# Attention and two gated layers on one core: the attention weights' transposition and product, three of eight last products, and one scale operand are changed

## The chip, the cores and the metric

The kernel runs on one core of a Trainium2 chip. The metric is the device time of one launch in microseconds (us). The engines are named as in the profile: PE is TensorE (matmuls; PEld is its weight load), DVE is VectorE, ACT is ScalarE, POOL is GpSimd, SP is SyncE, which here only issues DMAs. Each engine takes its own instructions strictly in their written order, and waits on semaphores for the others.

## The reference

Attention of 12288 queries over 768 pooled keys (keys and values are the same matrix), then two layers of width 2048, the first with a leaky ReLU of its own slope for each column, the second with a rational function.

```python
kv_pool = kv.reshape(B, H // r, r, W // r, r, C).mean(axis=(2, 4))      # 768 x 128
k = v = kv_pool.reshape(B, -1, C) @ w_sr
s = (q @ k.transpose(0, 2, 1)) / np.sqrt(C)
a = np.exp(s - s.max(-1, keepdims=True))
a /= a.sum(-1, keepdims=True) + 1e-09
x = a @ v                                                               # 12288 x 128
h = x @ w_in                                                            # 128 -> 2048
x = (np.maximum(h, 0.0) + alpha * np.minimum(h, 0.0)) @ w_out           # 2048 -> 128
h = x @ w_in2
P = a[0] + a[1]*h + a[2]*h*h + a[3]*h*h*h
Q = 1.0 + np.abs(b[0]) * np.abs(h) + np.abs(b[1]) * h*h
out = (P / (Q + 1e-6)) @ w_out2
```

## The kernel before

The work is cut in three streams that run beside each other for most of the launch.

**Attention.** 96 tiles `t` of 128 queries. A tile's scores are two halves of 384 keys (`S_half`), DVE writes them negated with the running minimum (`S_neg`), ACT takes the exponential (`S_exp2`), and POOL multiplies by the reciprocal sum (`norm`). The normalized weights `e` (128 queries x 768 keys) then have to stand with the keys on the partitions. PE transposes them in six blocks of 128 (`T_pe`, three into one bank), ACT copies each three twice, to `aTh` (rounded to the type fp32r) and to `tf` (`T_hi`), and POOL subtracts to get the rest `aTl` (`T_lo`). Two tiles make a pair `g` (48 pairs). The product with the values (`AV`) is done in three terms for each of six blocks of keys, `vh*aTh`, `vh*aTl`, `vl*aTh`, 18 matmuls of 256 columns to a pair (`mm3`, which records lines 381 to 383). The first 12 tiles (`EARLY`) run with their own banks while the weights are prepared; there DVE subtracts and POOL has no part in it.

**First layer.** 24 chunks of 512 queries, each with 16 steps of 128 hidden columns: `G1a` (three fp32r matmuls of 512), ReLU on ACT, a split by ACT and POOL in 11 of 16 steps, and `G2a` (three fp32r matmuls, or one f32 matmul in the five other steps; an f32 matmul of 512 columns stands as two records of the trace).

**Second layer.** 192 pairs of steps `s`: `G1b` on PE, then on ACT `act_u` (absolute value) and `act_p1` (a3*h + a2), on POOL two operations to the denominator, on ACT a logarithm and an exponential, on DVE `dve_e`, `dve_p2`, `dve_p3`, `dve_gr`, and a last product. That is `dve_g` on DVE or, where `by_pool` says so, `act_f` on ACT and `pool_g` on POOL. Then comes `G2b`, an f32 matmul for each step, and each chunk leaves by a DVE transposition in blocks of 32 x 32 and four DMAs to a pair.

**What sets the order.** Every operation is an `Op` with an engine, a cost, a rank and its dependencies. `emit_in_time` goes through a planned time: it takes the operation that can start first, and by rank where several can, and writes it out. So each engine's order is fixed when the program is built, from the costs and from tables of numbers (`TR`, `WR`, `RT`, `RA`, `RB`, `SPREAD`, `LH`, `LM`, `LT`, `RK`). Buffers are rings (`BUFS`, `Ring`): `S` is one bank that holds in turn score halves, transposed weights and the AV product; `e` has 4 buffers. `add(..., port=True)` keeps DVE operations apart from POOL ones in the planned time.

Of the kernel before, what the change touches and what calls it, by code (L numbers as in the profile page):

```python
# [8 lines left out]
F32 = mybir.dt.float32  # L9
# [12 lines left out]
B = 32  # L22
LN2 = 0.6931471805599453
# [173 lines left out]
def kernel(  # L197
# [37 lines left out]
    GEND = (0, 1, 1, 1, 1, 0, 1, 1, 1, 0, 1, 1, 0, 1, 0, 1, 0, 0, 0, 0)  # L235
    FIRST = 0
    LAST = 0
    WR = (46.7, 55.28, 111.13, 125.65, 140.69, 248.67, 278.77, 278.99, 302.55, 429.42, 352.76, 380.94, 597.47, 591.71, 462.41, 295.52)
    TR = (21.24, 22.34, 24.58, 34.83, 72.31, 76.18, 101.27, 117.78, 121.37, 122.99, 130.89, 131.26)
    LH = (137.96, 75.92, 55.11)  # L240
    LM = 45.18
    LT = (44.51, 44.83, 42.99)
    TLO = (1, 1)
    XLO = 0
    TLE = (0, 0)
# [11 lines left out]
        relu=-99.63, G2a=43.29, u=46.57, p1=63.42, t=89.27, ln=107.53, ex=141.17, e=225.02, p2=69.42, p3=50.3, gr=-124.79, g=40.13, f=67.85, gp=39.2, G2b=28.14, gs=13.78, q=27.79,  # L257
# [3 lines left out]
        qraw=True, qf=1, qT=2, S=1, nm=4, sm=4, r=4, e=4, aT=2, xf=1, tf=3, x0=3,  # L261
# [33 lines left out]
    vh = const.tile([P, KB, P], F32R, name="vh")  # L295
    vl = const.tile([P, KB, P], F32R, name="vl")
# [69 lines left out]
    shared = dict(SHARE, qTh="qT", qTl="qT", aTh="aT", aTl="aT", x1h="x1", x1l="x1")  # L366
# [37 lines left out]
    with tc.manual_schedule():  # L404
# [131 lines left out]
        def kT_mm(h):  # L536
            ps = st["kT", h] = new("ps", "S2", [P, HK])
            nc.tensor.matmul(
                out=ps, lhsT=st["wsr"], rhs=st["pooled"][:, h * HK : h * HK + HK], start=True, stop=True
            )  # L540

        def kT_hi(h):
            copy(kTh[:, h * HK : h * HK + HK], st["kT", h], sc)

        def kT_lo(h):
            sl = slice(h * HK, h * HK + HK)
            nc.vector.scalar_tensor_tensor(
                out=kTl[:, sl], in0=st.pop(("kT", h)), scalar=sc, in1=kTh[:, sl],
                op0=ALU.mult, op1=ALU.subtract,
            )  # L550
# [20 lines left out]
        for b in range(KB):  # L571
# [4 lines left out]
            a = add("ACT", act_us(P), 31, lambda b=b: copy(vh[:, b, :], st["v", b]), p)  # L576
            l = add(
                "DVE", dve_us(P), 31,
                lambda b=b: nc.vector.tensor_tensor(
                    out=vl[:, b, :], in0=st.pop(("v", b)), in1=vh[:, b, :], op=ALU.subtract  # L580
                ), a,
            )
            d.append(l)
            v_ops += [a, l]

        def prep_small():
# [3 lines left out]
            nc.vector.tensor_scalar(out=nav, in0=av, scalar1=-1.0, scalar2=None, op0=ALU.mult)  # L590

# [6 lines left out]
        ]  # L598

# [293 lines left out]
        def T_pe(t, j, ring):  # L893
            ps = A["T", t, j] = new("aps", ring, [P, 3, P])
# [5 lines left out]
        def tlo(t, j):  # L900
            return (TLE if t < EARLY else TLO)[j]
# [11 lines left out]
        def T_lo(t, j):  # L913
            g, k = divmod(t, 2)
            sl = (slice(None), slice(None), slice(k * P, k * P + P))
            eng, src = (nc.gpsimd, "tf") if tlo(t, j) else (nc.vector, "T")
            eng.tensor_tensor(  # L917
                out=A["aTl", g, j][sl], in0=A.pop((src, t, j)), in1=A["aTh", g, j][sl],
                op=ALU.subtract,
            )  # L920

        def AV(g, part, ring):
            if part == 0:
                A["av", g] = new("aps", ring, [P, 2 * P])
            ah, al_ = A.pop(("aTh", g, part)), A.pop(("aTl", g, part))
            for k in range(3):
                b = 3 * part + k
                mm3(
                    A["av", g], vh[:, b, :], vl[:, b, :], ah[:, k, :], al_[:, k, :],
                    start=(b == 0), stop=(b == KB - 1),  # L930
                )

# [73 lines left out]
        def transposes(t):  # L1006
            rank = tile_rank(t) + RT
            ring = "T" if t < EARLY else "S"
            g, k = divmod(t, 2)
            n, d_e = s_ops.pop(t)  # L1010
            if k == 0:
                T_ops[g] = [[], []]
            for j in range(2):
                p = add("PE", 0.33, rank, lambda j=j: T_pe(t, j, ring), n)
                d_e.append(p)
                d = rings[ring].take(p)
# [533 lines left out]
```

## Time and profile before

| | |
|---|---|
| median of 3 runs | 1523.71 us (1522.19 to 1524.54) |
| span of the profiled execution | 1521.4 us; this is its own time, from the first to the last instruction, and the page gives no other |
| PE busy | 1482.4 us (97%) |
| DVE busy | 1433.0 us (94%) |
| ACT busy | 1424.4 us (94%) |
| POOL busy | 1326.4 us (87%) |
| mean granted TensorE clock | 0.993 of 2.4 GHz |

Four engines stand near the span, so the share over the whole span does not tell which of them the others wait for. The page's slices show that the first two fortieths and the last are different from the rest: there every engine has gaps. In the stretches between, PE's row has no gap, and the others' have. A PE record's duration overlaps with the next one's, so what a matmul costs is read from the distance between two starts and not from its duration.

### The profile page before, as it was taken

What the parts mean: (1) busy time and instruction counts of PE and PEld (TensorE: products, weight loads), DVE (VectorE), ACT (ScalarE), POOL (GpSimd) and SP (SyncE); (2) the same over time, 40 slices, a digit from 0 to 9 for tenths busy, and PEclk for the clock granted to TensorE, in tenths of its full rate; (3) what the DMA queues carried; (4) which work ended last, traced back from release to release, by engine and by line L of the source; (5) the groups of instructions that cost most, each with busy time, mean ns of one, the idle gap of its engine ahead of it and who ended that gap; (6) DMA issues with size and microseconds to landing.
All of it is one profiled execution on the core that took longest, in us unless ns stands there. A gap on an engine that the chain in (4) does not pass through costs nothing.

```text
span 1521.4 us, 20213 instructions
## 1 busy us (share of the span) xinstructions
PE 1482.4 (97%) x6372; PEld 1065.0 (70%) x6372; DVE 1433.0 (94%) x2161; ACT 1424.4 (94%) x2488; POOL 1326.4 (87%) x1005
## 2 busy tenths in 40 slices
PE   6899999999999999999999999999999999999995
PEld 5777777777777777767777776777777776777652
DVE  5999999999999999999999999999999999999996
ACT  3969999999999999999999999999999999999996
POOL 0258999999999999989999989899999898899997
PEclk9999999999999999999999999999999999999997
DMA  8320000000000000000000000000000000000000
GB/s 285 91 63 0 8 14 1 15 14 1 15 10 5 14 8 8 14 8 8 14 1 15 5 10 15 1 14 8 8 14 8 0 8 8 1 8 8 1 14 7
DMA packets 102411, 28.65 MB, mean 19 GB/s; under 512 B 92960, under 2 KB 99744, under 8 KB 102304
## 3 DMA queue, kind: packets, MB, share of 16 engines
q1 hardware_dynamic: 102192, 27.35, 7.7%
q8 instruction: 50, 0.82, 0.2%
q0 software_dynamic: 112, 0.01, 0.1%
q14 instruction: 57, 0.47, 0.1%
HBM read 21.05 MB, written 6.29 MB: 18 GB/s over the span
## 4 chain that ended last, share of the span: by engine, by line
PE 86%; DVE 5%; ACT 4%; POOL 3%; issue 1%; DMA 1%; SPq 0%; DVEq 0%; POOLq 0%; ACTq 0%
PE acc L1302 20%; PE h L381 11%; PE h L383 11%; PE h L382 11%; PE acc L1157 6%; PE acc L381 4%; PE acc L383 4%; PE acc L382 4%; PE S L381 4%; PE S L382 4%; PE S L383 4%; PE S L898 4%; DVE work L615 1%; POOL work L1263 1%; POOL work L1210 1%
## 5 line engine op out<-in xcount | busy, mean ns | idle before, releaser
L1210 POOL TENSOR_TENSOR work<-work 128x1024 f32<-128x1024 f32 x192 | 460.4, 2398 | 8.0
L1302 PE MATMUL acc<-work,wo 128*128 128x512 f32 x768 | 393.7, 600 | 10.1 <-POOL work L1263 9.4
L1196 ACT ACTIVATE work<-h,nav 128x512 f32<-128x512 f32 x384 | 319.4, 840 | 2.2 <-PE h L383 1.2
L1141 POOL TENSOR_TENSOR rl<-work,rh 128x512 fp32r<-128x512 f32 x216 | 281.0, 1301 | 38.0 <-ACT rh L1132 34.7
L1240 DVE SCALAR_TENSOR_TENSOR work<-work,nav,h 128x512 f32<-128x512 f32 x384 | 281.8, 741 | 4.0
L1236 DVE TENSOR_TENSOR work<-work,h 128x512 f32<-128x512 f32 x384 | 258.8, 679 | 22.8 <-ACT work L1196 21.4
L1203 POOL TENSOR_SCALAR work<-work,bab 128x1024 f32<-128x1024 f32 x192 | 231.4, 1205 | 36.3 <-ACT work L1191 21.4
L1191 ACT ACTIVATE work<-h 128x512 f32<-128x512 f32 x384 | 247.0, 646 | 11.5 <-PE h L383 9.0
L1230 DVE SCALAR_TENSOR_TENSOR work<-work,rp 128x1024 f32<-128x1024 f32 x192 | 233.2, 1214 | 21.7 <-ACT rp L1223 19.3
L1248 DVE SCALAR_TENSOR_TENSOR rp<-work,nav,rp 128x1024 f32<-128x1024 f32 x181 | 231.6, 1280 | 0.0
L1120 ACT ACTIVATE work<-h 128x512 f32<-128x512 f32 x336 | 215.1, 640 | 13.5 <-PE h L383 11.1
L1269 DVE SCALAR_TENSOR_TENSOR work<-work,rp 128x1024 f32<-128x1024 f32 x181 | 219.6, 1213 | 1.8
L1215 ACT ACTIVATE work<-work 128x1024 f32<-128x1024 f32 x192 | 213.9, 1114 | 7.0 <-POOL work L1210 5.0
L1223 ACT ACTIVATE rp<-work 128x1024 f32<-128x1024 f32 x192 | 207.7, 1082 | 8.2 <-DVE work L1269 3.7
L381 PE MATMUL h<-x,w1h 128*128 128x512 f32 x384 | 202.4, 527 | 2.3 <-ACT work L1120 1.2
L381 PE MATMUL h<-x1h,w2h 128*128 128x512 f32 x384 | 187.1, 487 | 3.8 <-DVE work L1240 3.8
L1302 PEld LDWEIGHTS acc<-work,wo 128*128 128x128 f32 x768 | 141.3, 191 | 61.8 <-issue 26.3
L917 POOL TENSOR_TENSOR aTl<-tf,aTh 128x384 fp32r<-128x384 f32 x168 | 170.2, 1019 | 9.4 <-ACT tf L386 9.1
L383 PE MATMUL h<-x1h,w2l 128*128 128x512 f32 x384 | 151.8, 395 | 0.0
L383 PE MATMUL h<-x,w1l 128*128 128x512 f32 x384 | 151.7, 395 | 0.0
L382 PE MATMUL h<-x1l,w2h 128*128 128x512 f32 x384 | 151.3, 394 | 0.0
L382 PE MATMUL h<-x,w1h 128*128 128x512 f32 x384 | 151.1, 393 | 0.0
(138 smaller groups left out, 3226.2 us busy)
## 6 DMA issues: line engine op xcount, KB each, us to landing
work<-in_kv_dram SPq DMA_DIRECT2D x12, 512.0 KB, 8.7
out_dram<-work SPq DMA_DIRECT2D x184, 32.0 KB, 1.6
qraw<-in_q_dram SPq DMA_DIRECT2D x80, 64.0 KB, 2.3
work<-in_moe_w_out_dram SPq DMA_DIRECT2D x8, 512.0 KB, 4.4
work<-in_moe_w_in_dram SPq DMA_DIRECT2D x8, 512.0 KB, 4.5
qraw<-in_q_dram SPq DMA_DIRECT2D x4, 256.0 KB, 2.9
out_dram<-work SPq DMA_DIRECT2D x2, 128.0 KB, 1.8
work<-in_w_sr_dram SPq DMA_DIRECT2D x1, 64.0 KB, 7.9
```

Source lines behind the costliest of these rows:

```text
L381: nc.tensor.matmul(out=ps, lhsT=wh, rhs=xh, start=start, stop=False)
L382: nc.tensor.matmul(out=ps, lhsT=wh, rhs=xl, start=False, stop=False)
L383: nc.tensor.matmul(out=ps, lhsT=wl, rhs=xh, start=False, stop=stop)
L1141: nc.gpsimd.tensor_tensor(out=E["rl", s], in0=E.pop(("r1", s)), in1=E["rh", s], op=ALU.subtract)
L1191: nc.scalar.activation(out=E["u", s][:, k, :], in_=E["h2", s + k], func=AF.Abs)
L1196: nc.scalar.activation(out=E["p1", s][:, k, :], in_=E["h2", s + k], func=AF.Identity, scale=nav[:, 3:4], bias=nav[:, 2:3],)
L1210: nc.gpsimd.tensor_tensor(out=t, in0=t, in1=E.pop(("u", s)), op=ALU.mult)
L1230: nc.vector.scalar_tensor_tensor(out=t, in0=t, scalar=QEPS, in1=E["r0", s], op0=ALU.add, op1=ALU.mult)
L1236: nc.vector.tensor_tensor(out=p, in0=p, in1=E["h2", s + k], op=ALU.mult)
L1240: nc.vector.scalar_tensor_tensor(out=p, in0=p, scalar=nav[:, 1:2], in1=E.pop(("h2", s + k)), op0=ALU.add, op1=ALU.mult,)
L1248: nc.vector.scalar_tensor_tensor(out=E["gr", s], in0=p, scalar=nav[:, 0:1], in1=r, op0=ALU.add, op1=ALU.mult)
L1302: nc.tensor.matmul(out=E["acc2", i], lhsT=wo[2][:, KEEP[2].index(j), :], rhs=E["g", s][:, k, :], start=st_, stop=sp,)
```

## The change

The change takes the transposition of the normalized weights off PE, ACT and POOL for tiles 12 to 95. DVE transposes `e` in blocks of 32 x 32 in one instruction of 768 elements (`T_dve`), and four DMAs on SP's queue bring the blocks to their partitions (`T_place`). To make these DMAs contiguous, the keys are numbered otherwise from the pooling on (`kv_out`, `kT_mm`, `kT_hi`). The first 12 tiles still go through PE, with one ACT copy each and no subtraction.

The AV product has one f32 matmul in place of three fp32r ones: 6 to a pair in place of 18. `vl` is gone.

`by_pool` says yes for three of eight pairs of steps (`GPAT`) outside the last 20, where `GEND` decided before and still does with other entries. In all it is 75 of 192 pairs after and 11 before.

`act_p1` takes its scale from a register of ScalarE, loaded once, in place of a column of `nav`.

All tables that set the order have other numbers, and `FPAT` has the same eleven split steps at other places.

```diff
-    RT = 12.37
-    RA = 14.54
-    RB = 119.19
-    SPREAD = 30.17
+    RT = 23.26
+    RA = 19.89
+    RB = 256.57
+    SPREAD = 25.96
...
+    GPAT = (0, 1, 0, 0, 1, 0, 0, 1)
...
-        def T_hi(t, j):
-            g, k = divmod(t, 2)
-            if k == 0:
-                A["aTh", g, j] = new("at", "aTh", [P, 3, 2 * P], F32R)
-                A["aTl", g, j] = new("at", "aTl", [P, 3, 2 * P], F32R)
-            copy(A["aTh", g, j][:, :, k * P : k * P + P], A["T", t, j])
-            if tlo(t, j):
-                A["tf", t, j] = new("at", "tf", [P, 3, P])
-                copy(A["tf", t, j], A.pop(("T", t, j)))
...
+        def T_dve(t):
+            A["eb", t] = new("at", "eb", [P, NK])
+            nc.vector.transpose(out=A["eb", t], in_=A.pop(("e", t)))
+
+        def T_place(t):
+            to, eb = land(t), A.pop(("eb", t))
+            for a in range(W4):
+                nc.sync.dma_start(
+                    out=to[:, a].rearrange("p k i -> p (k i)"),
+                    in_=eb[a * B : a * B + B].rearrange("j (w n) -> j w n", w=W4),
+                )
...
-            for k in range(3):
-                b = 3 * part + k
-                mm3(
-                    A["av", g], vh[:, b, :], vl[:, b, :], ah[:, k, :], al_[:, k, :],
+            for b in range(3 * part, 3 * part + 3):
+                nc.tensor.matmul(
+                    out=A["av", g], lhsT=vf[:, b, :], rhs=A["eT", g][:, :, b, :],
                     start=(b == 0), stop=(b == KB - 1),
                 )
...
-                scale=nav[:, 3:4], bias=nav[:, 2:3],
+                scale=a3_reg, bias=nav[:, 2:3],
...
-            return k < len(GEND) and GEND[k]
+            return GEND[k] if k < len(GEND) else GPAT[s // 2 % len(GPAT)]
```

The order on PE in the middle of the program, before: `h` is a first product (`G1a` or `G1b`), `acc` a second one, and `S<-aTh,vh` begins an AV product.

```order
L381 MATMUL h_7545<-x1h,w2h 128x512
L382 MATMUL h_7545<-x1l,w2h 128x512
L383 MATMUL h_7545<-x1h,w2l 128x512
L1302 MATMUL acc_7032<-work,wo_67 128x512
L381 MATMUL S<-aTh,vh 128x256
L382 MATMUL S<-aTl,vh 128x256
L383 MATMUL S<-aTh,vl 128x256
```

Five more such threes follow there before the next `h`. PE after the change, at an AV product of the same stretch:

```order
L381 MATMUL h_6720<-x_5652,w1h 128x512
L382 MATMUL h_6720<-x_5652,w1h 128x512
L383 MATMUL h_6720<-x_5652,w1l 128x512
L938 MATMUL S<-eT,vf 128x256 x3
L381 MATMUL h_6737<-x1h,w2h 128x512
L382 MATMUL h_6737<-x1l,w2h 128x512
L383 MATMUL h_6737<-x1h,w2l 128x512
L938 MATMUL S<-eT,vf 128x256 x3
```

The 18 short matmuls have become two threes of f32 matmuls with a first product between them, and no `S<-ident,e` (a transposition) stands in the stretch any more. The first of the six waits for the DMAs of both tiles.

The order on DVE in the middle, before: a score pass (`e,nm<-S`), the steps of the second layer, and the last product (line 1269).

```order
L1248 SCALAR_TENSOR_TENSOR rp<-work,nav,rp 128x1024
L863 TENSOR_SCALAR e,nm<-S,nm 128x384
L1269 SCALAR_TENSOR_TENSOR work<-work,rp 128x1024
L877 TENSOR_SCALAR r<-sm 128x1
L882 RECIPROCAL r<-r 128x1
L445 STREAM_TRANSPOSE qf<-qraw 128x512
L1236 TENSOR_TENSOR work<-work,h_6796 128x512
L1240 SCALAR_TENSOR_TENSOR work<-work,nav,h_6796 128x512
```

DVE after the change; line 1264 is the old 1248, and where it writes `work` in place of `rp` the last product that followed is POOL's.

```order
L1246 SCALAR_TENSOR_TENSOR work<-work,rp 128x1024
L1264 SCALAR_TENSOR_TENSOR work<-work,nav,rp 128x1024
L1252 TENSOR_TENSOR work<-work,h_6176 128x512
L924 STREAM_TRANSPOSE eb<-e 128x768
L1256 SCALAR_TENSOR_TENSOR work<-work,nav,h_6176 128x512
L1252 TENSOR_TENSOR work<-work,h_6184 128x512
L1256 SCALAR_TENSOR_TENSOR work<-work,nav,h_6184 128x512
```

A last product of 1024 elements is missing behind line 1264, and a transposition of 768 stands among the steps.

The order on SP's queue in the middle, before (each `x4` is one load of queries in blocks, each `x8` the results of a chunk):

```order
L436 DMA qraw_4366<-in_q_dram 32x16x32 x4
L1340 DMA out_0_dram<-work_88 32x8x32 x8
L436 DMA qraw_5152<-in_q_dram 32x16x32 x4
L1340 DMA out_0_dram<-work_88 32x8x32 x8
L436 DMA qraw_5618<-in_q_dram 32x16x32 x4
```

SP's queue after the change:

```order
L929 DMA eT_4516<-eb_4510 128x1x192 x4
L1356 DMA out_0_dram<-work_87 32x8x32 x8
L929 DMA eT_4819<-eb_4671 128x1x192 x4
L929 DMA eT_4819<-eb_4798 128x1x192 x4
L436 DMA qraw_5002<-in_q_dram 32x16x32 x4
L929 DMA eT_5076<-eb_4956 128x1x192 x4
```

Four DMAs for each tile (336 in all) now stand between the loads of queries and the results, in one queue that is worked off in order. At the queue's head one load of `moe_w_in` now stands ahead of the first loads of `q` and `kv`.

## Rows read from the trace of the kernel before

**Rows 1.** The page's part 1: span, busy time of each engine.

```profile
span 1521.4 us, 20213 instructions
PE 1482.4 (97%) x6372; PEld 1065.0 (70%) x6372; DVE 1433.0 (94%) x2161; ACT 1424.4 (94%) x2488; POOL 1326.4 (87%) x1005
```

**Rows 2.** Windows: stretch, length, busy of PE, PEld, DVE, ACT, POOL, clock, DMA.

```profile
150.00:1450.00 1300.00, 1300.00 (x5555) 934.60 (x5554) 1248.59 (x1842) 1260.47 (x2196) 1201.32 (x906) 1.00 0.05 9
800.00:850.00 50.00, 50.00 (x218) 36.33 (x217) 49.36 (x75) 49.14 (x86) 46.26 (x35) 1.00 0.07 11
```

**Rows 3.** Timeline of PE, two short stretches: start us, duration us, line, operation.

```profile
615.60 1.02 PE L1302 MATMUL acc<-work,wo 128*128 128x512 f32 x2
616.46 0.49 PE L898 MATMUL S<-ident,e 128*128 128x128 f32 x3
616.70 0.48 PE L381 MATMUL acc<-rh,wo1h 128*128 128x512 f32 x1
617.02 0.39 PE L382 MATMUL acc<-rl,wo1h 128*128 128x512 f32 x1
617.25 0.40 PE L383 MATMUL acc<-rh,wo1l 128*128 128x512 f32 x1
...
655.84 0.28 PE L381 MATMUL S<-aTh,vh 128*128 128x256 f32 x1
655.96 0.28 PE L382 MATMUL S<-aTl,vh 128*128 128x256 f32 x1
656.08 0.28 PE L383 MATMUL S<-aTh,vl 128*128 128x256 f32 x1
```

**Rows 4.** Groups by line: shapes and count, busy us, mean ns, idle before.

```profile
L1230 DVE SCALAR_TENSOR_TENSOR work<-work,rp 128x1024 f32<-128x1024 f32 x192 | 233.2, 1214 | 21.7 <-ACT rp L1223 19.3 <-POOL aTl L917 0.8 <-POOL work L1210 0.3
L1236 DVE TENSOR_TENSOR work<-work,h 128x512 f32<-128x512 f32 x384 | 258.8, 679 | 22.8 <-ACT work L1196 21.4 <-ACT work L1191 0.6
L1269 DVE SCALAR_TENSOR_TENSOR work<-work,rp 128x1024 f32<-128x1024 f32 x181 | 219.6, 1213 | 1.8
L917 DVE TENSOR_TENSOR aTl<-T,aTh 128x384 fp32r<-128x384 f32 x24 | 12.9, 547 | 0.4 <-ACT aTh L386 0.2
L1196 ACT ACTIVATE work<-h,nav 128x512 f32<-128x512 f32 x384 | 319.4, 840 | 2.2 <-PE h L383 1.2 <-POOL work L1263 0.6 <-DVE rp L1248 0.4
L1191 ACT ACTIVATE work<-h 128x512 f32<-128x512 f32 x384 | 247.0, 646 | 11.5 <-PE h L383 9.0 <-POOL work L1210 1.0
L386 ACT ACTIVATE tf<-S 128x384 f32<-128x384 f32 x168 | 92.3, 549 | 0.0
L386 ACT ACTIVATE aTh<-S 128x384 fp32r<-128x384 f32 x168 | 90.6, 539 | 1.4 <-PE S L898 1.4
L1259 ACT ACTIVATE work<-work 128x1024 f32<-128x1024 f32 x11 | 11.8, 1077 | 0.8 <-DVE work L1230 0.8
L917 POOL TENSOR_TENSOR aTl<-tf,aTh 128x384 fp32r<-128x384 f32 x168 | 170.2, 1019 | 9.4 <-ACT tf L386 9.1
L1263 POOL TENSOR_TENSOR work<-work 128x1024 f32<-128x1024 f32 x11 | 26.1, 2380 | 1.4 <-ACT work L1120 1.0 <-DVE work L1248 0.4
```

**Rows 5.** One line's instructions: count, duration ns min/median/max, first and last start.

```profile
L445 DVE STREAM_TRANSPOSE qf<-qraw x20: 691/703/712, 69.6 to 1188.4; 128x512 f32<-128x512 f32 x20
...
L615 DVE TENSOR_SCALAR work<-work x48: 399/420/1922, 27.8 to 134.5; 128x512 int32<-128x512 int32 x32, 128x512 f32<-128x512 f32 x16
```

**Rows 6.** Timeline of DVE and POOL around one transposition.

```profile
401.17 1.04 POOL L917 TENSOR_TENSOR aTl<-tf,aTh 128x384 fp32r<-128x384 f32 x1
...
401.85 0.70 DVE L445 STREAM_TRANSPOSE qf<-qraw 128x512 f32<-128x512 f32 x1
```

**Rows 7.** The page's DMA issues (KB each, us to landing), and an issue.

```profile
out_dram<-work SPq DMA_DIRECT2D x184, 32.0 KB, 1.6
qraw<-in_q_dram SPq DMA_DIRECT2D x80, 64.0 KB, 2.3
...
1480.02 1.93 SPq L1340 DMA_DIRECT2D out_dram<-work  x4
```

More of the change, by code (lines that the diff above doesn't have):

```diff
@@ L22 @@
 B = 32
+W4 = P // B
 LN2 = 0.6931471805599453
@@ L575 @@
             d_pooled.append(p)
[L576 to L584, printed above, removed]
+            a = add("ACT", act_us(P), 31, lambda b=b: copy(vf[:, b, :], st.pop(("v", b))), p)
+            d.append(a)
+            v_ops.append(a)
         def prep_small():
@@ L598 @@
         ]
+        a3_op = add(
+            "ACT", 0.2, 7, lambda: nc.scalar.reg_load(a3_reg, nav[0:1, 3:4].bitcast(I32)), small[0]
+        )
         def f64_to_f32(src, k, dst, rank, dst_ring=None):
@@ L1011, in transposes @@
             if k == 0:
[L1012 to L1016, printed above, removed]
-                h = add("ACT", act_us(HK) * (1 + tlo(t, j)), rank, lambda j=j: T_hi(t, j), p)
-                if k == 0:
-                    d_aT[g, j] = rings["aT"].take(h)
-                else:
-                    h.after(T_ops[g][j][0])
-                eng = "POOL" if tlo(t, j) else "DVE"
-                l = add(eng, tt_us(eng, HK), rank, lambda j=j: T_lo(t, j), h)
-                if tlo(t, j):
-                    rings["tf"].take(h).append(l)
-                last = h if tlo(t, j) else l
-                d.append(last)
-                T_ops[g][j] += [h, l]
-        d_aT = {}
+                T_ops[g] = []
+            if t < EARLY:
+                first = None
+                for j in range(2):
+                    p = add("PE", 0.33, rank, lambda j=j: T_pe(t, j), n)
+                    d_e.append(p)
+                    d = rings["T"].take(p)
+                    h = add("ACT", act_us(HK), rank, lambda j=j: T_copy(t, j), p, first)
+                    d.append(h)
+                    first = first or h
+                    T_ops[g].append(h)
+            else:
+                x = add("DVE", dve_us(NK), rank, lambda: T_dve(t), n)
+                d_e.append(x)
+                d_eb = rings["eb"].take(x)
+                first = add("SP", 1.6, rank, lambda: T_place(t), x)
+                d_eb.append(first)
+                T_ops[g].append(first)
+            if k == 0:
+                d_eT[g] = rings["eT"].take(first if t >= EARLY else T_ops[g][0])
+                lead_T[g] = T_ops[g][0]
+            else:
+                (first if t >= EARLY else T_ops[g][-2]).after(lead_T.pop(g))
+        d_eT, lead_T = {}, {}
         def outputs(g):
@@ L1429, in moe2 @@
                 p1 = add(
-                    "ACT", act_us(w, ptrs=2), stage(st, "p1"), lambda k=k: act_p1(s, k), g1, *p3s
+                    "ACT", act_us(w, ptrs=1), stage(st, "p1"), lambda k=k: act_p1(s, k), g1, a3_op, *p3s
                 )
```

86 lines of the change are left out of this document (47 added, 39 removed).

## The prediction

> **What bounds the kernel now.** I read the page's busy times first [rows 1]. PE has 1482.4 of 1521.4 us, DVE 1433.0, ACT 1424.4, POOL 1326.4: four engines within 13 points, so the page alone does not name the bound. The windows do [rows 2]. From 150 to 1450 us PE is busy for 1300.00 of 1300.00 us at the full clock (1.00, that is 2.4 GHz), while DVE has 1248.59 (96.0%), ACT 1260.47 (97.0%) and POOL 1201.32 (92.4%). PE's 39.0 us without work (1521.4 - 1482.4) all lie outside, in the start, where the attention of the first tiles and the weights' preparation are done, and in the last 70 us.
>
> A full PE row can still hide waits, because a matmul's modelled duration overlaps the next start. So I take distances between starts [rows 3]. An fp32r matmul of 512 columns takes 617.25 - 617.02 = 0.23 us, although its row says 0.39. An f32 matmul of 512 (two records) takes 616.46 - 615.60 = 0.86. Three transpositions and the next two matmuls take 617.25 - 616.46 = 0.79, less 2 x 0.23 leaves 0.33 for the three. An fp32r matmul of 256 takes 0.12. These are about what a queue that never waits would show, and they follow one another without a hole in both pieces. So in the middle each microsecond taken off PE's queue is a microsecond of the span, as long as no other engine becomes the later one.
>
> **The change, part by part.** *PE, transpositions.* Tiles 12 to 95 lose six each: 84 x 2 threes x 0.33 = -55.4 us.
>
> *PE, the AV product.* 18 fp32r matmuls of 256 go, 48 pairs x 18 x 0.12 = -103.7 us. Six f32 matmuls of 256 come. The trace has none, so I take half of the f32 matmul of 512, 0.43, because in fp32r halving the columns halves the distance as well (0.23 to 0.12): 48 x 6 x 0.43 = +123.8. Net +20.1. The bound below is this value, since columns cannot stream faster; the bound above is 0.48, if each carries 0.05 of fixed cost as a short instruction may, which adds 14 us. I keep 0.43. PE in sum: -55.4 + 20.1 = -35.3 us, with -21 as the poorer end.
>
> *DVE.* Added are 84 transpositions of 768 elements. The trace has them at 512: median 703 ns [rows 5]. Going from 512 to 1024 elements costs 1214 - 679 = 535 ns on this engine [rows 4], so 256 more cost 267 and one takes 0.97 us: +81.5 us. The ends are 0.70 (59 us) and one and a half times 703, 1.05 (89 us). Removed are the last products that POOL takes over: 75 - 11 = 64 of 1213 ns [rows 4], -77.6 us. The 24 early subtractions go too, -12.9. Net -9.0, and DVE comes to about 1424 us. In the middle, where the early ones are not, it is +3.9: 1248.6 to 1252.5 us.
>
> The Trainium skill, "VectorE: DVE Perf Modes", section "The three transpose paths", gives 311 ns for a 128 x 128 block on VectorE. An estimate by that page would be 6 x 0.311 = 1.87 us for a tile, 157 us in all, and DVE would become the bound with some 75 us more. The row speaks against it: four blocks in one instruction took 703 ns, not 1244 [rows 5], since the fixed part is paid once. The sum stays with the row.
>
> *ACT.* Both copies of the transposed weights go, 92.3 + 90.6 = -182.9 us [rows 4]. The 64 further `act_f` cost 1077 ns each, +68.9. `act_p1` now takes 840 ns with two operands from columns, `act_u` 646 with none [rows 4]; with one I take the middle, 743: 384 x -97 = -37 us (0 to -74). Net about -151. ACT falls to some 1273 us and stops being a neighbour of the bound. So the exact price of the register does not matter to the time.
>
> *POOL.* -170.2 for the subtractions, 64 x 2380 ns = +152.3 for the products [rows 4]: -18 us, to about 1308.
>
> *SP and the placement.* 336 DMAs join the queue that carries the loads of queries and the results. Four issues take 1.93 us, and landings take 1.6 us (32 KB) to 2.3 us (64 KB from memory, in small pieces) [rows 7]. I take 2.3 for these 96 KB, so `AV` can start about 1.5 + 2.3 = 3.8 us after the transposition (bounds 3.0 and, with the landing doubled, 6.1). This lies beside PE's other streams, which have two layers' matmuls ready. What would stand behind a late placement on PE's queue is everything, because the first AV matmul of a pair waits for both tiles' eight DMAs; and on SP's queue it is the query loads. If every pair waited, each microsecond of wait would cost 48 - 6 = 42 us.
>
> *The bank `S`.* A pair used it for four score halves, four threes of transposed weights and the AV product; the four threes go. It comes free earlier, which removes short waits of PE. I give it nothing, since PE shows no idle time there.
>
> *Start and end.* DVE loses 12.9 us of early work, but a load of `moe_w_in` now goes ahead of `kv`, and its conversion ahead of the first pooling on DVE. 512 KB more in front is some 2 us. I count 0 (-8 to +6). The end has the same chain of second-layer steps; 0 again, -5 to +5.
>
> **The sum.** If PE stays the only bound, the span is 1521.4 - 35.3 = 1486.1 us. Then DVE would have 1252.5 us in a middle of 1300 - 35.3 = 1264.7, which is 99.0%. The fullest slice of 50 us that I found has 49.36, 98.7% [rows 2]. At 98.7% the middle would be 1269, 4 us more. I take these 4: span 1490.1. The runs' median lies 2.3 us above the profiled span (1523.71 against 1521.4), so the forecast is 1492.4, rounded 1492 us.
>
> **The rivals.**
>
> *A. DVE becomes the bound.* For it: DVE needs 99% where it had 96.0%, and it waits on ACT and POOL inside a pair of steps. Against: ACT, which ended most of DVE's waits (the 21.4 and 19.3 us in [rows 4]), gets 151 us lighter, so the 50 us that DVE waited in the middle should shrink. At 97.5% the middle is 1285 us, 15 below today: 1521.4 - 15 + 2.3 = 1509. At 96.3% nothing would be gained. I give 1500 to 1515 a chance of 0.20.
>
> *B. The placement comes late (the other side).* PE waits at each AV product for the last of eight DMAs. 35.3 / 42 = 0.84 us of wait for each pair eats the gain. At 2 us it is 42 x 2 - 35 = +49, about 1573 us. For it: the SP queue is in order, and a result that waits for its chunk holds up the placement behind it. The order gives no comfort beyond its own plan: it writes the AV product no sooner than 0.2 + 1.6 + 2.8 = 4.6 us of planned time after the transposition (`SEEN` and the cost of `T_place`). Against: that is 0.8 us more than the 3.8 worked out above, and a landing of 3.9 us in place of 2.3 would be needed to reach the threshold. Chance 0.09, from the threshold upwards.
>
> *C. DVE's transpositions and POOL lock each other out.* The early `tensor_scalar` operations show such a thing: 420 ns in the median, 1922 at most [rows 5], once POOL works as well. If the transposition had to wait for POOL's running instruction, about half of 1201.32 / 906 = 1.33 us in nine cases of ten, it would cost 84 x 0.6 = 50 us on DVE, and the span would be some 1560. Against: all 20 transpositions of today lie between 691 and 712 ns, and the one shown ran for its 0.70 us across a POOL subtraction [rows 5, 6]. Chance 0.03. The Trainium skill, "SBUF — State Buffer", section "Who interferes with whom", names copy, cast and tensor_scalar as what can take the pair of ports that VectorE shares with GpSimd, and not transpositions; by that rule C does not happen here, and the trace agrees (691 to 712 ns).
>
> *D. More than forecast.* DVE's relief in the start shortens it, and the emptier `S` bank and ACT let the tail close up: 8 + 5 us, and PE alone the bound: 1486 - 13 + 2.3 = 1475. Chance 0.09 for 1465 to 1481.
>
> *E. The change does not do what it says:* the saved time comes back as short waits on all engines, since DVE, PE and POOL are all above 92%, and the time ends between 1515 and today's. For it: in the middle POOL would be at (1201.3 - 18) / 1265 = 93.5%, and a last product on POOL takes 2380 ns where DVE takes 1213, so results come later. Against: the output buffers hold five products. Chance 0.04.
>
> **Numbers.** My forecast (1481 to 1500) has 0.55, A 0.20, B 0.09, C 0.03, D 0.09, E 0.04. Time 1492 us. The range 1475 to 1515 leaves out B, C, E and half of D, that is 0.16 + 0.04. About 0.2% (3 us) is what this measurement can tell from no change. Faster is the forecast, A, D and half of E, 0.86; the same is the rest of E and a sliver of B, 0.03; slower is most of B and C, 0.11.
>
> **What the changed profile would show.** Right: PE without gaps in the middle, `S<-eT` starts 0.43 us apart, `eb<-e` at 0.97 us, DVE's share in the middle 98 to 99%, ACT near 84% of the span and POOL near 88%. A would show PE waiting for `h2` banks that DVE's third product frees, with DVE at 97% there. B would show PE waiting on DMAs at `S<-eT`; C would show `eb<-e` far above 1 us, or POOL instructions stretched beside it. What makes the forecast wrong most easily is the dear end of the f32 matmul of 256 or a start that got longer by more than 6 us.

## The result, and the profile after

The changed kernel takes 1488.46 us (median of 4 runs, 1485.47 to 1490.16), against 1524.12 us (1522.19 to 1524.85) for the kernel before, measured beside it. The ratio is 0.9767, 95% interval 0.9756 to 0.9779: 35.7 us less. The forecast was 1492 us, from 1475 to 1515.

The page of the changed kernel, the span and the busy times of the engines, answers to [rows 1]:

```profile
span 1484.9 us, 18574 instructions
PE 1444.2 (97%) x5580; PEld 1026.1 (69%) x5580; DVE 1407.3 (95%) x2151; ACT 1333.2 (90%) x2216; POOL 1311.7 (88%) x901
```

PE has 38.2 us less than in [rows 1], and its time without work is 1484.9 - 1444.2 = 40.7 us, where it was 39.0. So the gain lies in PE's work and not in its holes. The windows of the changed kernel (start and end, their length, then PE, PEld, DVE, ACT and POOL busy, the granted clock, the DMA share and GB/s) answer to [rows 2]:

```profile
150.00:1415.00 1265.00, 1264.97 (x4813) 898.23 (x4812) 1232.38 (x1845) 1174.11 (x1929) 1192.82 (x806) 1.00 0.16 33
1415.00:1485.00 70.00, 51.29 (x128) 24.92 (x126) 56.80 (x66) 50.05 (x68) 55.35 (x29) 0.87 0.06 11
```

PE's row is full up to 1415 us, as it was up to 1450 us in [rows 2], at the same full clock (1.00 of 2.4 GHz). DVE is at 1232.38 of 1265, 97.4% (96.0% before), POOL at 94.3%, and ACT has dropped from 97.0 to 92.8%.

An AV product on PE's timeline, in the middle (start, duration, instruction):

```profile
817.77 0.40 PE L383 MATMUL h<-x1h,w2l 128*128 128x512 f32 x1
818.01 2.75 PE L938 MATMUL S<-eT,vf 128*128 128x256 f32 x12
820.41 0.58 PE L381 MATMUL h<-x,w1h 128*128 128x512 f32 x1
820.83 0.40 PE L382 MATMUL h<-x,w1h 128*128 128x512 f32 x1
```

Six f32 matmuls are twelve records. From the first of them to the second matmul of the next product it takes 820.83 - 818.01 = 2.82 us; less 0.23 for the one fp32r matmul of 512 columns in between [rows 3], that is 2.59, or 0.43 for each of the six. No gap stands ahead of them or behind. By [rows 3] the eighteen fp32r matmuls of a pair took 18 x 0.12 = 2.16.

The line groups of the changed kernel (count, busy time, mean ns of one, idle time before them and who ended it) answer to [rows 4]:

```profile
L1252 DVE TENSOR_TENSOR work<-work,h 128x512 f32<-128x512 f32 x384 | 257.9, 678 | 17.4 <-ACT work L1212 15.6 <-ACT work L1207 0.4
L1246 DVE SCALAR_TENSOR_TENSOR work<-work,rp 128x1024 f32<-128x1024 f32 x192 | 232.5, 1211 | 10.5 <-ACT rp L1239 8.6 <-POOL work L1279 0.7
L1285 DVE SCALAR_TENSOR_TENSOR work<-work,rp 128x1024 f32<-128x1024 f32 x117 | 141.7, 1211 | 1.1
L924 DVE STREAM_TRANSPOSE eb<-e 128x768 f32<-128x768 f32 x84 | 81.5, 970 | 1.8 <-POOL e L896 1.7
L1212 ACT ACTIVATE work<-h,nav 128x512 f32<-128x512 f32 x384 | 270.9, 712 | 2.4 <-POOL work L1279 1.3 <-PE h L383 0.8
L1207 ACT ACTIVATE work<-h 128x512 f32<-128x512 f32 x384 | 235.0, 613 | 24.7 <-PE h L383 16.9 <-POOL work L1226 5.4
L1275 ACT ACTIVATE work<-work 128x1024 f32<-128x1024 f32 x75 | 81.3, 1084 | 1.2 <-DVE work L1246 1.0
L1279 POOL TENSOR_TENSOR work<-work 128x1024 f32<-128x1024 f32 x75 | 179.7, 2396 | 25.2 <-ACT work L1275 18.6 <-DVE work L1264 5.2 <-DVE r L890 1.3
```

`T_dve` (L924) costs 970 ns and 81.5 us, as worked out. DVE's waits for ACT in the first two groups are 15.6 and 8.6 us, where they were 21.4 and 19.3. The last products on POOL cost 2396 ns each, and POOL waits 18.6 us for the `act_f` in front of them.

What the trace says of the landing buffer `eT` (matmuls that read it; the placement's DMAs; time to landing), and the line group of the matmuls that read it, whose last number is PE's idle time before them:

```profile
L938 PE MATMUL S<-eT,vf x576: 377/379/383, 51.4 to 1366.8; 128*128 128x256 f32 x192
L929 SPq DMA_DIRECT2D eT<-eb x336: 542/603/1677, 109.7 to 1316.6; - x168
...
DMA to landing us min/median/max: 2.3/2.4/4.2
...
L938 PE MATMUL S<-eT,vf 128*128 128x256 f32 x576 | 137.6, 379 | 0.0
```

The landing takes 2.4 us in the median (forecast 2.3) and 4.2 at most. PE has no idle time before an AV matmul: the row of L938 ends in 0.0. The placement is hidden.

### The profile page after: what moved, and what is told of

Read it like the earlier page. It is cut to its first block, busy times and chain, and to the rows that moved or that the text cites. A ratio compares the mean times of both kernels' runs of the same rounds, so it can differ in the third digit from the quotient of the medians.

```text
span 1484.9 us, 18574 instructions
## 1 busy us (share of the span) xinstructions
PE 1444.2 (97%) x5580; PEld 1026.1 (69%) x5580; DVE 1407.3 (95%) x2151; ACT 1333.2 (90%) x2216; POOL 1311.7 (88%) x901
## 4 chain that ended last, share of the span: by engine, by line
PE 88%; DVE 6%; POOL 2%; ACT 2%; issue 1%; DMA 1%; POOLq 0%; SPq 0%; DVEq 0%; ACTq 0%
PE acc L1318 20%; PE h L381 11%; PE h L383 11%; PE h L382 11%; PE S L938 8%; PE acc L1173 6%; PE acc L383 4%; PE acc L381 4%; PE acc L382 4%; PE S L381 2%; PE S L382 2%; PE S L383 2%; PE m L499 1%; DMA work<-in_kv_dram 1%; DVE work L1246 1%
## 5 line engine op out<-in xcount | busy, mean ns | idle before, releaser
L1226 POOL TENSOR_TENSOR work<-work 128x1024 f32<-128x1024 f32 x192 | 460.0, 2396 | 9.4
L1256 DVE SCALAR_TENSOR_TENSOR work<-work,nav,h 128x512 f32<-128x512 f32 x384 | 279.0, 736 | 2.1
L1252 DVE TENSOR_TENSOR work<-work,h 128x512 f32<-128x512 f32 x384 | 257.9, 678 | 17.4 <-ACT work L1212 15.6
L1212 ACT ACTIVATE work<-h,nav 128x512 f32<-128x512 f32 x384 | 270.9, 712 | 2.4 <-POOL work L1279 1.3
L1207 ACT ACTIVATE work<-h 128x512 f32<-128x512 f32 x384 | 235.0, 613 | 24.7 <-PE h L383 16.9
L1246 DVE SCALAR_TENSOR_TENSOR work<-work,rp 128x1024 f32<-128x1024 f32 x192 | 232.5, 1211 | 10.5 <-ACT rp L1239 8.6
L1136 ACT ACTIVATE work<-h 128x512 f32<-128x512 f32 x336 | 205.8, 613 | 34.5 <-PE h L383 31.7
L1239 ACT ACTIVATE rp<-work 128x1024 f32<-128x1024 f32 x192 | 202.1, 1053 | 20.4 <-DVE work L1285 17.6
L1231 ACT ACTIVATE work<-work 128x1024 f32<-128x1024 f32 x192 | 207.2, 1079 | 8.9 <-POOL work L1226 5.4
L381 PE MATMUL h<-x,w1h 128*128 128x512 f32 x384 | 209.6, 546 | 1.1 <-ACT rh L1148 0.7
L1279 POOL TENSOR_TENSOR work<-work 128x1024 f32<-128x1024 f32 x75 | 179.7, 2396 | 25.2 <-ACT work L1275 18.6
L381 PE MATMUL h<-x1h,w2h 128*128 128x512 f32 x384 | 196.4, 511 | 2.6 <-DVE work L1256 2.6
L1318 PEld LDWEIGHTS acc<-work,wo 128*128 128x128 f32 x768 | 145.6, 191 | 70.0 <-issue 30.7
L382 PE MATMUL h<-x,w1h 128*128 128x512 f32 x384 | 151.1, 393 | 0.0
L1264 DVE SCALAR_TENSOR_TENSOR rp<-work,nav,rp 128x1024 f32<-128x1024 f32 x117 | 149.6, 1279 | 0.0
L1285 DVE SCALAR_TENSOR_TENSOR work<-work,rp 128x1024 f32<-128x1024 f32 x117 | 141.7, 1211 | 1.1
```

What stands on the lines that cost most here:

```text
L381: nc.tensor.matmul(out=ps, lhsT=wh, rhs=xh, start=start, stop=False)
L382: nc.tensor.matmul(out=ps, lhsT=wh, rhs=xl, start=False, stop=False)
L1207: nc.scalar.activation(out=E["u", s][:, k, :], in_=E["h2", s + k], func=AF.Abs)
L1212: nc.scalar.activation(out=E["p1", s][:, k, :], in_=E["h2", s + k], func=AF.Identity, scale=a3_reg, bias=nav[:, 2:3],)
L1226: nc.gpsimd.tensor_tensor(out=t, in0=t, in1=E.pop(("u", s)), op=ALU.mult)
L1246: nc.vector.scalar_tensor_tensor(out=t, in0=t, scalar=QEPS, in1=E["r0", s], op0=ALU.add, op1=ALU.mult)
```

## The experiments

The kernel before took 1524.1 to 1525.7 us in the four sets of runs. A difference named "against the changed kernel" is to its 1488.46 us. The small ones of 7 to 8 us are clear of the noise: their ratios to the kernel before have intervals that do not meet the changed kernel's 0.9756 to 0.9779. Kernels made from the changed one keep its tables unless their text says otherwise. So what they lose can in part be an order that was made for other work. Theory 1, the prediction's, is that PE's queue sets the time, with DVE close behind. The rivals are that the gain comes from somewhere else (DVE's relief, the start and end, the order), and that something hidden (the placement, ACT) in truth has a price.

**1. AV in f32 alone, in the kernel before.** ACT's second copy and POOL's subtraction go with it.

```diff
-                mm3(
-                    A["av", g], vh[:, b, :], vl[:, b, :], ah[:, k, :], al_[:, k, :],
+                nc.tensor.matmul(
+                    out=A["av", g], lhsT=vf[:, b, :], rhs=ah[:, k, :],
...
```

> The kernel before with one part of the change alone: the AV product in f32 (6 matmuls to a pair in place of 18), transpositions still on PE, one ACT copy each and no subtraction. If PE's queue alone is the bound: 48 x (6 x 0.43 - 18 x 0.12) = +20 us, about 1544 us, although ACT loses 168 copies (some 62 us by distances between starts of 0.37) and POOL 170 us. If the four engines bind each other: the relief of ACT and POOL shows, 1524 or less.

Measured: 1545.42 us, ratio 1.0134 (1.0116 to 1.0152), 19.7 us slower than before. The page's busy times:

```profile
PE 1501.9 (97%) x6084; PEld 1074.4 (70%) x6084; DVE 1426.0 (92%) x2131; ACT 1376.0 (89%) x2320; POOL 1165.1 (75%) x837
```

POOL lost 161 us, ACT 48 and DVE 7 against [rows 1], and yet the time rose by what PE's busy time rose (19.5 us). That is the prediction's +20.1 for the AV product, and it shows that this kernel, with the tables of before, follows PE's queue although the others have less to do.

**2. The transpositions back on PE, in the changed kernel.** The late tiles go through the bank `S` and one ACT copy again, with the old `RT` and `RA`. They meet the values in another order of keys than the reference's; the work is the same.

```diff
-            if t < EARLY:
+            ring = "T" if t < EARLY else "S"
+            if True:
                 first = None
...
```

> The changed kernel with the transpositions of all tiles on PE again (one ACT copy each, no DVE transposition, no placement DMAs; the two ranks RT and RA of before, since transposed weights share the bank S again). If PE's queue is the bound: 168 threes x 0.33 = +55 us, about 1543 us. If DVE had become the bound in the changed kernel: its 81 us of transpositions go, and the time rises by much less than 55, to 1505 or below.

Measured: 1551.53 us, ratio 1.0173 (1.0154 to 1.0191), 63 us above the changed kernel. The page:

```profile
PE 1504.2 (97%) x6084; PEld 1072.1 (69%) x6084; DVE 1359.4 (88%) x2067; ACT 1393.9 (90%) x2384; POOL 1311.8 (85%) x901
```

The forecast for these transpositions was 55.4 us. PE's busy time rose by 60.0, although DVE got 48 us lighter. Runs 1 and 2 together carry the sum: +20 and -55 to -63.

**3. Less and more on PE: is it still the bound?** In one kernel the AV product takes three of six blocks of keys, so half of the values are left out. In the other, three further matmuls go into the same bank and are overwritten. The planned costs and so the order stay as they are.

```diff
-            for b in range(3 * part, 3 * part + 3):
+            for b in range(3 * part, 3 * part + 3 * (part == 0)):
...
+            for b in (0, 1, 2) if part == 0 else ():
+                nc.tensor.matmul(
+                    out=A["av", g], lhsT=vf[:, b, :], rhs=A["eT", g][:, :, b, :],
...
```

> The changed kernel with the AV product over three of the six blocks of keys only (half of the values are left out), all else as it is. It takes 48 x 3 x 0.43 = 62 us from PE and from no other engine. If PE were the bound with room below it: 1426 us. If DVE stands right behind it (1232 us in the middle, 98.7% as the most that a slice showed): the middle can shrink from 1265 to 1249 only, about 1472 us. If DVE is the bound already: 1485 to 1488.

> The changed kernel with three further f32 matmuls of 256 in each AV product, whose sums are overwritten by the product itself. It puts 62 us on PE and nothing on another engine. If PE's queue is the bound, the whole of it shows: about 1550 us. If PE had slack behind DVE, less: 1530 or below.

Measured: with half the product 1481.72 us (ratio 0.9715, 0.9697 to 0.9734), only 6.7 us below the changed kernel. With half as much again 1545.54 us (1.0144, 1.0122 to 1.0165), 57 us above it. So PE is the bound upwards, at 57 us for some 62 us of work. Downwards, with the order as it is, something else takes over a little under the present time. The weight loads in front of the first products show what. First the kernel with half the product, then the changed kernel:

```profile
L381 PEld LDWEIGHTS h<-x1h,w2h 128*128 128x128 f32 x384 | 72.2, 188 | 72.6 <-DVE work L1256 50.2 <-issue 5.8 <-ACT work L1212 1.7
L381 PEld LDWEIGHTS h<-x,w1h 128*128 128x128 f32 x384 | 72.1, 188 | 104.2 <-ACT rh L1148 46.0 <-ACT work L1136 29.4 <-DVE rl L1140 8.5
```

```profile
L381 PEld LDWEIGHTS h<-x1h,w2h 128*128 128x128 f32 x384 | 72.5, 189 | 44.0 <-DVE work L1256 19.5 <-issue 10.0 <-DVE e L871 1.0
L381 PEld LDWEIGHTS h<-x,w1h 128*128 128x128 f32 x384 | 72.2, 188 | 60.4 <-ACT rh L1148 22.5 <-ACT work L1136 14.7 <-issue 10.3
```

With PE 62 us lighter, PE's weight loads wait for the banks that DVE's third product (L1256) and ACT's roundings and ReLU (L1148, L1136) free: both engines hold it, DVE with 50.2 us and ACT with 46.0 and 29.4. The stretch from 150 to 1400 us of this kernel:

```profile
150.00:1400.00 1250.00, 1223.81 (x4524) 834.14 (x4523) 1220.54 (x1832) 1161.56 (x1913) 1183.67 (x800) 1.00 0.16 34
```

PE has gaps here (97.9%), and DVE is at 97.6%. Whether DVE and ACT are at their limit there, or an order fitted to the lighter PE would gain more, is not shown.

**4. No last product on GpSimd outside the last 20.**

```diff
-    GPAT = (0, 1, 0, 0, 1, 0, 0, 1)
+    GPAT = (0, 0, 0, 0, 0, 0, 0, 0)
```

> The changed kernel with the last products outside the last 20 pairs of steps on DVE again (GpSimd keeps those that the table of the end gives it). DVE gets 64 x 1.13 = +72 us, ACT loses some 60 and POOL some 150. If DVE stands right behind PE: its middle of 1232 + 72 = 1304 us at 98.7% makes 1321, 56 more than now, about 1544 us. If PE alone is the bound and DVE has room: 1488.

Measured: 1551.94 us, ratio 1.0180 (1.0163 to 1.0197), 63.5 us above the changed kernel. The page, a line group and the middle:

```profile
PE 1469.5 (95%) x5580; PEld 1023.0 (66%) x5580; DVE 1480.2 (96%) x2215; ACT 1297.2 (84%) x2152; POOL 1165.9 (75%) x837
...
L1219 POOL TENSOR_SCALAR work<-work,bab 128x1024 f32<-128x1024 f32 x192 | 231.0, 1203 | 160.7 <-DVE work L1285 132.4 <-DVE r L890 8.8 <-ACT work L1212 7.2
...
150.00:1400.00 1250.00, 1234.14 (x4663) 867.23 (x4661) 1228.29 (x1818) 1074.66 (x1775) 989.05 (x709) 1.00 0.16 34
```

DVE has 72.9 us more. It is at 98.3% of the middle, where PE now has gaps (98.7%), and POOL waits 132.4 us for DVE's last products. The sum with DVE as the bound gave 1544 us, 8 less than measured. So this is in the main rival A, come true in a kernel that has the transposition on DVE and not the handing over of last products; how much of the 63.5 us comes from tables that were made for 75 last products on POOL is not shown. With these tables PE's 36 us are to be had only with both parts.

**5. Eight placement DMAs for a tile, of 48 KB, in place of four of 96.**

```diff
             for a in range(W4):
+                for c in range(2):
...
```

> The changed kernel with eight placement DMAs of 48 KB for each tile in place of four of 96 KB, the order unchanged. The last one is issued about 4 x 0.48 = 1.9 us later. If the placement is hidden behind PE's other work: 1488 within 3 us. If the AV product waits for it: up to 42 x 1.9 = 80 us more, and PE is seen to wait at S<-eT.

Measured: 1487.50 us (1485.09 to 1487.95), ratio 0.9758 (0.9742 to 0.9774): no different from the changed kernel. 336 issues more on SP cost nothing, and each of the smaller DMAs lands after 2.0 us in the median. Rival B's wait is not there, and SP's queue has room.

**6. The scale of `act_p1` from a column again.**

```diff
-                scale=a3_reg, bias=nav[:, 2:3],
+                scale=nav[:, 3:4], bias=nav[:, 2:3],
```

> The changed kernel with the scale of act_p1 from the column again, the order unchanged. ACT gets 384 x 0.09 to 0.13, 35 to 50 us, at 90% of the span. If ACT is off the path: 1488 within 3 us. If it takes part in the bound: some 15 to 35 us more.

Measured: 1496.69 us, ratio 0.9815 (0.9799 to 0.9832), 8.2 us above the changed kernel. Two line groups and the middle, then the middle of the changed kernel:

```profile
L1212 ACT ACTIVATE work<-h,nav 128x512 f32<-128x512 f32 x384 | 308.5, 811 | 1.8 <-POOL work L1279 1.1 <-PE h L383 0.5
L381 PEld LDWEIGHTS h<-x,w1h 128*128 128x128 f32 x384 | 72.1, 188 | 81.6 <-ACT rh L1148 34.1 <-ACT work L1136 26.1 <-issue 7.7
...
150.00:1400.00 1250.00, 1249.23 (x4728) 876.34 (x4727) 1211.17 (x1816) 1177.52 (x1891) 1171.19 (x792) 1.00 0.16 34
```

```profile
150.00:1400.00 1250.00, 1249.97 (x4759) 888.06 (x4758) 1217.49 (x1825) 1159.12 (x1906) 1177.92 (x796) 1.00 0.16 34
```

ACT has 30 us more in all (1363.3 of busy time). The weight loads of `G1a` waited for ACT 22.5 and 14.7 us in the changed kernel, and 34.1 and 26.1 here. An engine with 10% of its time free still holds PE. PE's row does not show it: it is as good as full in both (1249.23 and 1249.97 of 1250), but in the same 1250 us PE gets through 4728 records where the changed kernel gets through 4759. A full PE row can hide waits, and the count of matmuls in a stretch shows them.

**7. The changed kernel with all tables of before.** `WM`, which before did not exist, is the later of a pair of `WR`, as the code of before had it.

```diff
-    RT = 23.26
+    RT = 12.37
...
-        relu=6.03, G2a=54.48, u=10.88, p1=95.75, t=136.76, ln=392.42, ex=361.17, e=604.29, p2=31.84, p3=-13.01, gr=-134.44, g=32.45, f=110.86, gp=30.78, G2b=37.06, gs=508.8, q=-280.41,
+        relu=-99.63, G2a=43.29, u=46.57, p1=63.42, t=89.27, ln=107.53, ex=141.17, e=225.02, p2=69.42, p3=50.3, gr=-124.79, g=40.13, f=67.85, gp=39.2, G2b=28.14, gs=13.78, q=27.79,
```

> The changed kernel with the tables of the kernel before (ranks, leads, weights' order, the end's table, the places of the split steps); the three of eight stay. If the gain is the work taken off PE: 1488 to 1503. If it is the refitted order: 1515 or more.

Measured: 1542.60 us, ratio 1.0119 (1.0102 to 1.0136). This is 54 us above the changed kernel and 18 us slower than before. Of the two branches of the expectation the second came, that of the order. The same operations in the old order give the whole gain back and more.

**8 to 10. Which table?** Each of these has one part of the old numbers: the ranks inside a second-layer pair (`RK`); the weights and the first 12 tiles (`WR`, `WM`, `TR`); how far the first layer runs ahead (`LH`, `LM`, `LT`). The attention's own pace (`RT`, `RA`, `RB`, `SPREAD`) was not run alone. The edit of the third:

```diff
-    LH = (272.09, 61.63, 55.65)
-    LM = 46.92
-    LT = (46.31, 45.79, 44.45)
+    LH = (137.96, 75.92, 55.11)
+    LM = 45.18
+    LT = (44.51, 44.83, 42.99)
```

> The changed kernel with the numbers of before in one table alone: the ranks of the operations inside a second-layer pair of steps. With all tables of before it took 1542.6 us, 54 more than the changed kernel. If the loss is of that table (a last product on GpSimd needs an operand from ScalarE, which the old ranks do not foresee), 1520 to 1545 us, with VectorE and GpSimd waiting for ScalarE in the middle. If the loss is spread over all tables, some 1495 to 1510. If these ranks hardly matter, 1486 to 1492.

> The changed kernel with the numbers of before for the weights' preparation and the first 12 attention tiles alone. With all tables of before TensorE was busy for 90 us between 50 and 150 us, 6.5 less than in the changed kernel. If only the start is touched, the loss is these 6 or 7 us and no more: 1493 to 1497 us, with the middle and the end as in the changed kernel. If the preparation sets when the second layer can begin and so the end too, 1505 or more. Unchanged: 1486 to 1490.

> The changed kernel with the numbers of before for how far the first layer runs ahead of the second alone. With all tables of before the last 91 us after 1450 us held 57.6 us of TensorE work, so some 33 us of it were idle, against some 14 in the changed kernel. If this table sets how the end closes up, 1500 to 1520 us, the loss after 1415 us. If it does not, 1486 to 1492 (most of its numbers moved by two units or less).

Measured, against the changed kernel: the ranks +50.6 us (1539.07; ratio 1.0103, 1.0086 to 1.0121), the weights +25.6 (1514.10; 0.9937, 0.9921 to 0.9954), the lead +8.1 (1496.53; 0.9829, 0.9812 to 0.9846). The first two came out in the branch of their expectation with the larger loss; the lead's time lies between its two branches. They do not add up: 84 us in sum, 54 all together. The middle of the kernel with the old ranks (window) and three of its waits there, from 150 to 1400 us (engine, line, who ended it, us in total, times, longest):

```profile
150.00:1400.00 1250.00, 1228.70 (x4612) 857.05 (x4612) 1175.17 (x1774) 1119.16 (x1835) 1131.32 (x769) 1.00 0.16 34
```

```profile
DVE work L1252 <- ACT work L1212: 41.0, 44, 4.4
...
ACT work L1231 <- POOL work L1226: 27.6, 35, 2.1
...
POOL work L1219 <- ACT work L1207: 39.3, 34, 2.9
```

And the same three waits in the changed kernel:

```profile
DVE work L1252 <- ACT work L1212: 13.6, 24, 1.9
...
ACT work L1231 <- POOL work L1226: 4.9, 7, 1.5
...
POOL work L1219 <- ACT work L1207: 5.4, 8, 2.0
```

No engine is full: PE 98.3%, DVE 94.0%, POOL 90.5%, ACT 89.5%. With the old ranks, what ACT computes in front of DVE (`act_p1`, L1212) and of POOL (`act_u`, L1207) comes late for them, and ACT's logarithm (L1231) waits longer for POOL's denominator (L1226), though all three have time to spare. The three waits grow from 23.9 to 107.9 us. Nothing but the ranks differs, so the loss is of the order.

The old numbers for the weights cost 25.6 us. The stretch from 50 to 150 us, first with them, then in the changed kernel:

```profile
50.00:100.00 50.00, 45.48 (x229) 37.72 (x228) 33.09 (x70) 40.33 (x83) 17.37 (x19) 0.97 0.25 60
100.00:150.00 50.00, 44.35 (x188) 32.11 (x187) 46.66 (x99) 36.73 (x71) 31.23 (x30) 1.00 0.35 85
```

```profile
50.00:100.00 50.00, 47.64 (x252) 39.70 (x251) 43.01 (x88) 47.24 (x100) 19.10 (x23) 1.00 0.37 95
100.00:150.00 50.00, 49.23 (x210) 37.18 (x209) 47.79 (x98) 41.07 (x78) 39.00 (x33) 1.00 0.17 38
```

PE loses 7 us there, and DVE, ACT and POOL 9.5 to 11 each. Work that is late on the three engines behind PE has to be done later, when they have little room; that would make the loss more than PE's. The trace fits: from 150 to 1400 us PE gets through 4715 records with the old numbers and 4759 in the changed kernel, 0.9% less, which by this share is some 12 of the other 18 us. Where the rest lies was not followed further, and the cause is argued, not tested.

**11. A further step split in the first layer, on ScalarE.** The expectation counts one step too many: this table splits 12 of 16 steps, not 13. So 24 products on PE change, for 24 x 0.17 = 4 us less, and ACT has 72 roundings more (168 before, 240 now), 48 of them in place of POOL's.

```diff
-    FPAT = (4, 2, 0, 4, 1, 4, 0, 4, 0, 4, 1, 4, 0, 2, 4, 0)
+    FPAT = (4, 4, 0, 4, 1, 4, 4, 4, 0, 4, 1, 4, 0, 4, 4, 0)
```

> The changed kernel with 13 in place of 11 of 16 first-layer steps split (two f32 products of 0.86 us become three of 0.23 us in each of 24 chunks: 48 x 0.17 = 8 us less on TensorE), with all roundings on ScalarE (some 46 us more there) and 48 more subtractions on GpSimd, less 48 roundings (some 32 us more). If TensorE alone sets the time, 1480 us. If ScalarE stands as near behind it as the scale from a column showed (30 us more work there cost 8 us), 1488 to 1502: nothing gained, or slower.

Measured: 1496.52 us, ratio 0.9819 (0.9802 to 0.9835), 8.1 us above the changed kernel. ACT has 1365.8 us of busy time, 32.6 more. By PE alone it would have gained 4; the 30 us more on ACT cost as much as in experiment 6. No kernel here that does the whole of the work is faster than the changed one.

## Why the prediction was right, and where not

**The bound and PE's sum held.** PE was forecast at -35.3 us; its busy time fell by 38.2, the runs by 35.7. Both terms were tested apart: the AV product +20.1 forecast, +19.7 measured; the transpositions -55.4 forecast, 63 measured when they return, with a second engine loaded by the same step (ACT +60.7), so that this is the size within some 8 us. The f32 matmul of 256 columns, for which the trace of before had no row, was taken at 0.43 and shows 0.43 in the AV product above; its dear end of 0.48 did not come. No row showed the 0.05 us of fixed cost in that end, and none shows it now.

**DVE's transposition was right to the digit**: 0.97 us and 81.5 us, from the row at 512 elements [rows 5] and the price of 256 more [rows 4]. That price was taken between rows of two different operations, so the last digit owes something to luck. All 84 transpositions, and one of them with the instruction behind it:

```profile
L924 DVE STREAM_TRANSPOSE eb<-e x84: 957/970/980, 108.6 to 1311.3; 128x768 f32<-128x768 f32 x84
...
824.81 0.97 DVE L924 STREAM_TRANSPOSE eb<-e 128x768 f32<-128x768 f32 x1
825.70 0.70 DVE L1256 SCALAR_TENSOR_TENSOR work<-work,nav,h 128x512 f32<-128x512 f32 x1
```

They lie between 957 and 980 ns, so no instruction of POOL held one up (rival C). The Trainium skill's 311 ns for a 128 x 128 block ("VectorE: DVE Perf Modes", section "The three transpose paths") is a figure for bf16, where these blocks are f32, and the prediction did not say so. It does not carry over to six blocks in one instruction: six times 311 ns would be 1.87 us, and the trace has 0.97.

**DVE's total was 17 us too high** (1424 forecast, 1407.3 measured). The three terms that were counted come out as forecast if durations are added: +81.5, -77.9 (219.6 less 141.7 for the last products) and -12.9. But DVE's neighbours overlap too: the transposition above lasts 0.97 us, and the next instruction starts after 0.89. In the busy time the terms weigh less. Experiment 2 takes the 84 transpositions out, and DVE's busy time falls by 47.9 us, not 81.5; experiment 4 gives 64 last products back for 72.9; experiment 1, without the early subtractions, has 7.0 less. 47.9 - 72.9 - 7.0 = -32, where the forecast said -9 and the profiles differ by -25.7. The 6 us between -32 and -25.7 are not traced.

**The 4 us allowed for DVE were not needed**: the span is 1484.9, where PE alone gave 1486.1. DVE came to 97.4%, not to 98 to 99%. But that DVE stands close behind PE was judged rightly. Half an AV product more off PE gives 6.7 us instead of 62 (experiment 3), and without POOL's share DVE sets the time (experiment 4). Rival D's 1475 us was not reached by PE's relief alone: in this order even a PE 62 us lighter gives 1481.7.

**ACT was mis-sized**: forecast 1273, measured 1333.2 (POOL, forecast at 1308, has 1311.7). The step that failed is "-182.9" for the copies, and with it +68.9 for `act_f`: both multiply durations. (The -37 for the register came close: experiment 6 gives 30.1.) ACT's neighbours overlap, so a copy in a dense row takes less of the busy time than its duration. The timeline of ACT in the kernel before shows it:

```profile
808.08 0.55 ACT L386 ACTIVATE aTh<-S 128x384 fp32r<-128x384 f32 x1
808.45 0.56 ACT L386 ACTIVATE tf<-S 128x384 f32<-128x384 f32 x1
808.82 0.67 ACT L1191 ACTIVATE work<-h 128x512 f32<-128x512 f32 x1
```

A copy lasts 0.55 us, but the next start comes after 0.37. Experiments 1 and 2 give the copies' weight in the busy time, 48.4 and 60.7 us for 168 each; experiment 4 gives 36.0 for 64 `act_f`, experiment 6 gives 30.1 for the register. -48.4 - 60.7 + 36.0 - 30.1 = -103, where the forecast said -151 and the profiles differ by -91. For PE the prediction took distances between starts, for ACT and DVE it did not.

**"The exact price of the register does not matter to the time" was wrong.** It matters by 8.2 us (experiment 6). ACT did stop being at 97% (92.8% in the middle), but the weight loads of PE's first-layer products did not wait less for it. These loads in the kernel before:

```profile
L381 PEld LDWEIGHTS h<-x,w1h 128*128 128x128 f32 x384 | 72.2, 188 | 62.5 <-ACT work L1120 19.7 <-ACT rh L1132 18.7 <-issue 8.4
```

They waited 38.4 us for ACT's ReLU (L1120) and rounding (L1132) then, 37.2 in the changed kernel, and 60.2 in experiment 6.

**The step that was not there at all: the order.** The prediction moved time only by sums of work, and gave the refitted tables nothing. Experiments 7 to 10 show that the sums are a floor which the old order misses by 54 us, so that the same change with the old tables would have been slower than before. The forecast was right because the order of the changed kernel reaches the floor of PE. The prediction did not argue that from a row; in this point it was lucky. It could have asked: the old ranks stood beside 11 last products on POOL, and 75 have to be fed by ACT now.

**Start, end and placement** were costed at nothing. PE is idle for 22 us in the first 150 us (20 before), and for 19 in the last 70 (19 before). The landing took 2.4 us.

**Open**: which of the 17 ranks carries the 50 us; how much the kernels of experiments 3 and 4 would gain by tables fitted to them; 6 us of DVE's fall and 12 of ACT's; and whether the new tables would also help the old kernel, which was not tried. That last one is a rival for a part of the gain. Against it: PE's row was full from 150 to 1450 us [rows 2], so that in this stretch new tables could win only what a full row hides, and the time without work outside is no shorter after the change (40.7 us, 39.0 before).

## What to carry to other kernels

When one engine has a full row, add up what a change takes off its queue by distances between starts; do the same, not durations, for every engine that stands behind it. Ask next how far the second engine is: here half an AV product less on PE gave 7 us before two other engines held it, so that with these tables the change is worth its 36 us only as a whole (without the handing over to GpSimd the kernel took 27 more than before). A full row of the first engine does not tell that it never waits; count its instructions in a stretch as well. And an order made for one distribution of work is not neutral for another: when work moves between engines, fit the order again before judging the change, and test old numbers in the new kernel to know what the order itself is worth.

## What the runs showed of the hardware that was not expected

A scale from a register of ScalarE was cheaper than one from a column by 0.10 us in an instruction of 512 elements; other sizes were not run. The changed kernel's ACT timeline, and behind it that of experiment 6:

```profile
823.48 0.69 ACT L1212 ACTIVATE work<-h,nav 128x512 f32<-128x512 f32 x1
824.05 0.61 ACT L1136 ACTIVATE work<-h 128x512 f32<-128x512 f32 x1
```

```profile
822.78 0.78 ACT L1212 ACTIVATE work<-h,nav 128x512 f32<-128x512 f32 x1
823.45 0.60 ACT L1136 ACTIVATE work<-h 128x512 f32<-128x512 f32 x1
```

From `act_p1`'s start to the next it is 0.57 us with the register and 0.67 with the column, so 384 x 0.10 = 38 us of ACT's queue, of which 30 show in its busy time and 8 reach the kernel's time. And 336 placements of 96 KB, which raised the DMA share of the middle from 0.05 to 0.16, hardly lengthened the 64 KB loads of queries: 2.4 us to landing in the median, and 2.3 before [rows 7].
